# Attention with a bilinear gate in one kernel: when split weights count as ready, when score banks count as free, and where the output weights are split

## The chip, the core and the metric

The kernel runs on one core of a Trainium2 chip. TensorE (PE), VectorE (DVE), ScalarE (ACT), GpSimd (POOL) and SyncE (SP, which only issues transfers here) work side by side and wait for one another through semaphores. The metric is the device time of one execution in microseconds; lower is better.

## The reference

The input x has 2048 rows of 576 values in float32. It is normalised row by row; the result xn goes through 32-head attention (head size 18) and through a bilinear unit of width 4608, and both meet in the output:

```python
    xn = _layernorm(x, axis=-1)
    s = _A_ref(xn, A_wqkv, A_wo)
    g = _silu(_B_ref(xn, B_w_gate, B_w_up, B_w_down))
    return x + s * g
# _A_ref: softmax(q k^T * Dh**-0.5) v, heads joined, @ wo
# _B_ref: h = (x @ w_gate) * (x @ w_up); h @ w_down
```

## The kernel before

**Splitting.** PE multiplies a rounded form of float32 (`fp32r`). To keep accuracy, each operand is split into a high part, which is a rounded copy made by ACT, and a low part, which is the difference, made by POOL or DVE. A product is then the sum of three of the four products of parts. Weights are split on the chip once and the split form is stored to DRAM, so that later passes only load it.

**Stages.** First the rows are normalised and transposed, q and k are computed (`qk_block`) and stored split to `sqk`, and v is computed in blocks of 128 rows (`v_block`): 28 matmuls into two PSUM banks, two ACT copies (L391) into a tile `vo`, and a store of it to `sv` (L393). There are three `vo` tiles, taken in turn. Four v blocks come early, eight later, then six q/k blocks of which the x columns are already on their way to the tile `xc` (L417), and then the last four v blocks.

The main stage runs four passes, one for each 512 rows. A pass has 18 units of 256 columns of the bilinear unit. A unit has two gate/up blocks of 27 matmuls (L618), which multiply x columns with the tile `wgu`, and then eight down blocks (L664), which multiply `hs` with the tile `wd` and add up into `acc`. Up uses one half of the array's rows, gate the other. Between them stand the scores: `a_item` (L530) computes scores of which DVE takes the row maximum (L532), `b_item` (L569) computes them again, transposed, and ACT takes the exponential (L571), and `pv_group` (L580) multiplies with v. Each kind of score has two PSUM banks; the other products share four.

Finally the attention's rows are transposed and multiplied with the output weights (L1187), scaled by the gate and added to x.

**What sets the order.** Everything is ordered by hand while the program is built. A planner keeps two clocks `clk`, one for each half of the array, a time `free` for DVE, ACT and POOL, and for each PSUM bank a time when it comes free. `pick` takes the next gate/up or down matmul that `can_go`, and scores are placed when their goal has come or nothing else can go. A score's bank is counted free 0.06 us after its reader's planned end.

**Small work.** The pieces of weight splitting stand in the list `chores`, other small work (the silu of finished rows) in `later`. At each step `small` may place one of them: for a piece on ACT, only if the planner thinks ACT free within 0.1 us.

```python
                if eng == "POOL" or free[eng] <= now + 0.1 + (0.15 * (now - quiet[0]) if q is later else 0.0):
```

When a block of products is placed whose weights have not been split yet, `gu_start` or `down_start` calls `ready`, which places all pieces ahead of it at once:

```python
    def ready(done, key):
        while key not in done:
            assert chores or later
            chore()
```

In pass 1, `g_get` makes the pieces of a gate/up block (three ACT copies L205, three POOL subtracts L206) and `d_get` those of a unit's down weights (two of each, L236 and L237). Their last entry, `end`, issues the store of the split weights and the load of the next raw ones on SP.

**Output weights.** `wo_prepare` is called with the last gate product. It loads them (L763, L765), and five ACT copies (L771) and five DVE subtracts (L772) split them.

Of the kernel before, what the change touches and what calls it, by code (L numbers as in the profile page):

```python
# [20 lines left out]
FT = mybir.dt.float32  # L21
FR = mybir.dt.float32r
# [18 lines left out]
def kernel(  # L41
# [10 lines left out]
    nc = tc.nc  # L52
# [23 lines left out]
    sv = dram.tile([S, H, DH + 1], FT, name="sv")  # L76
    so = dram.tile([S, D], FT, name="so")
    sg = dram.tile([S, D], FT, name="sg")

    turns = [0]  # L80

# [63 lines left out]


    chores, later = [], []

    def chore(all=True):
        q = (all and chores) or later  # L150
# [30 lines left out]
    def g_get(n):  # L181

        if n == 2 * len(units):
            u = n // 2 - 1
            dw[u] = wpool.tile([128, 2, 2, D], FR, name="wdl", tag="wgu", bufs=2)
            nc.sync.dma_start(dw[u].bitcast(FT), swd[columns_of(u)])
            ddone.add(u)
        if n >= 2 * len(units):
            return
        f = 2 * columns_of(n // 2) + n % 2  # L190
        if n > 1 and n // 2 % NF2 == 0:
            gw[n] = gw[n - 2]
            gdone.add(n)
            return
        w = gw[n] = g_tile()
        if n >= 2 * NF2:
            nc.sync.dma_start(w.bitcast(FT), swg[f])
            gdone.add(n)
            return
        if n not in graw:  # L200
            ready(gdone, n - 2)
        raw = graw.pop(n)

        def piece(b):
            nc.scalar.activation(w[:, b:b + 3, :], raw[:, b:b + 3, :], AF.Copy)  # L205
            nc.gpsimd.tensor_tensor(w[:, 9 + b:12 + b, :], raw[:, b:b + 3, :], w[:, b:b + 3, :].bitcast(FT),  # L206
                                    op=OP.subtract)

        def end():
            gdone.add(n)  # L210
            nc.sync.dma_start(swg[f], w.bitcast(FT))
            g_load(n + 2)

        chores.extend([(piece, (b,)) for b in (0, 3, 6)] + [(end, ())])
# [5 lines left out]
    def d_get(n):  # L220
        if n >= len(units) - 1:
            return
        p = columns_of(n)
        if n and n % NF2 == 0:
            dw[n] = dw[n - 1]
            ddone.add(n)
            return
        w = dw[n] = d_tile()
        if n >= NF2:
            nc.sync.dma_start(w.bitcast(FT), swd[p])  # L230
            ddone.add(n)
            return
        raw = draw.pop(n)

        def piece(k):
            nc.scalar.activation(w[:, k, 0, :], raw[:, k], AF.Copy)  # L236
            nc.gpsimd.tensor_tensor(w[:, k, 1, :], raw[:, k], w[:, k, 0, :].bitcast(FT), op=OP.subtract)  # L237

        def end():
            ddone.add(n)  # L240
            nc.sync.dma_start(swd[p], w.bitcast(FT))
            d_load(n + 1)

        chores.extend([(piece, (k,)) for k in range(2)] + [(end, ())])

    R = 3 * DH
    PT = 13
# [106 lines left out]
                i, k = x_part(b, 0)  # L354
                nc.sync.dma_start(xg[i][r:r + 64, k:k + 2, :].bitcast(FT), sx[c, b])

    vbox = {}

    def v_fetch(h):
        raw = vp.tile([128, 5, HALF], FT, name="wvraw", bufs=1)  # L360
# [7 lines left out]
    def v_split(h):  # L368
        if h == 0:
            vbox["w"] = vp.tile([128, 10, D], FR, name="wv")  # L370
            for i in range(3):
                vbox[i] = vp.tile([128, H, DH + 1], FT, name=f"vo{i}")
                nc.gpsimd.memset(vbox[i], 1.0)
        raw, wv = vbox["raw"], vbox["w"]
        cs = slice(h * HALF, (h + 1) * HALF)
        for k, d, lo in ((0, 0, 4), (1, 1, 5), (2, 2, 6), (3, 3, 7), (4, 8, 9)):
            nc.scalar.activation(wv[:, d, cs], raw[:, k, :], AF.Copy)
            nc.gpsimd.tensor_tensor(wv[:, lo, cs], raw[:, k, :], wv[:, d, cs].bitcast(FT),
                                    op=OP.subtract)

    def v_block(t):
        c, r = divmod(t, 4)
        ps = [bank("g", 3), bank("g", 3)]
        for h in range(2):
            for n, (a, e) in enumerate(PAIRS):
                nc.tensor.matmul(ps[h][:, 0:HALF], xcs[c][:, e, r * 128:(r + 1) * 128],  # L386
                                 vbox["w"][:, a, h * HALF:(h + 1) * HALF], start=n == 0,
                                 stop=n == len(PAIRS) - 1)
        v = vbox[t % 3]
        for h in range(2):  # L390
            nc.scalar.activation(v[:, 16 * h:16 * h + 16, 0:DH],  # L391
                                 ps[h][:, 0:HALF].rearrange("p (a b) -> p a b", b=DH), AF.Copy)
        nc.sync.dma_start(sv[t * 128:(t + 1) * 128], v)  # L393
# [68 lines left out]
    for i in range(2):  # L462
        qs.append(stk.tile([128, S], FR, name=f"qs{i}"))
        ks.append(stk.tile([128, S], FR, name=f"ks{i}"))
        nc.gpsimd.memset(ks[i].bitcast(FT), 1.0)
    g_load(0)
    g_load(1)
    d_load(0)
# [29 lines left out]
    for t in range(4, 8):  # L498
        v_block(t)
        chore()  # L500
    assert n == 18
    pro.close()
    vstack.close()

# [7 lines left out]
    with ExitStack() as mid:  # L512
# [106 lines left out]
                             stop=k == len(TERMS) - 1)  # L619

        def up_end(n, ps):
            us[n] = mp.tile([128, 512], FT, name="us", bufs=1)
            nc.scalar.activation(us[n], ps, AF.Copy)  # L623

# [99 lines left out]
        def down_summed(u, s):  # L724
            c, q = units[u]
            if q == NF2 - 1 and c < NCH - 1:
                seen[c, s] = seen.get((c, s), 0) + 1
                if seen[c, s] == 2:
                    silu_store(4 * c + s)

        def silu(t, new, end):

# [25 lines left out]

        wos = {}

        def wo_prepare():
            raw = xcp.tile([128, 8, D], FT, name="wor", tag="xc")
            nc.sync.dma_start(raw[:, 0:4, :], wo[0:512, :].rearrange("(k p) c -> p k c", p=128))  # L763
            for b in (0, 64):
                nc.sync.dma_start(raw[b:b + 64, 4, :], wo[512:576, :])  # L765
            wos[0] = xcp.tile([128, 8, D], FR, name="wos", tag="xc")
            wos[1] = wpool.tile([128, 2, D], FR, name="wos2", tag="wgu", bufs=2)

            def piece(k):
                hi, lo = (wos[0][:, k, :], wos[0][:, 4 + k, :]) if k < 4 else (wos[1][:, 0, :], wos[1][:, 1, :])  # L770
                nc.scalar.activation(hi, raw[:, k, :], AF.Copy)  # L771
                nc.vector.tensor_tensor(lo, raw[:, k, :], hi.bitcast(FT), op=OP.subtract)  # L772

            chores.extend([(piece, (k,)) for k in range(5)])

        passed = {}

        def stream(r, kind):

            def glu(n):  # L780
                c, q = units[n // 2]
                box = []
                for k in range(len(TERMS)):
                    def work(k=k):
# [6 lines left out]
                        if k == len(TERMS) - 1:  # L791
                            (gate_end if r else up_end)(n, box[0])
                            if r and n == 2 * len(units) - 1:
                                wo_prepare()
                    end = (("DVE", 0.70) if r else ("ACT", 0.60)) if k == len(TERMS) - 1 else None
                    yield 0.229, k == 0, work, end, ("g", n, k), len(TERMS)

# [33 lines left out]
        clk, free = [0.0, 0.0], {"DVE": 0.0, "ACT": 0.0, "POOL": 0.0}  # L831
        banks = {"a": [0.0] * 2, "b": [0.0] * 2, "g": [0.0] * 4}
        turn = {"a": 0, "b": 0}

# [30 lines left out]
        def a_next(r=0):  # L865
# [7 lines left out]
            a_item(h, i, r)  # L873
            slot = turn["a"] % 2
            turn["a"] += 1
            banks["a"][slot] = engine("DVE", clk[r] + 0.45, 0.70) + 0.06
            clk[r] += 0.229
            na += 1
            if i == N - 1:
# [8 lines left out]
        def b_next(r=1):  # L888
# [10 lines left out]
            slot = turn["b"] % 2  # L899
            turn["b"] += 1  # L900
            end = engine("ACT", clk[r] + 0.45, 0.60)
            banks["b"][slot] = end + 0.06
            clk[r] += 0.229
            nb += 1
            if i % 4 == 3:
                due.append((h, i // 4, end + 0.1))

        KINDS = {"piece": ("ACT", 0.55), "first": ("ACT", 0.70), "second": ("DVE", 0.45), "inverse": ("DVE", 1.06)}

        quiet = [0.0]  # L910

        def small(now):

            q = chores or later
            if q is later and now < quiet[0]:
                return
            if q:
                eng, length = KINDS.get(q[0][0].__name__, ("POOL", 0.0))
                if eng == "POOL" or free[eng] <= now + 0.1 + (0.15 * (now - quiet[0]) if q is later else 0.0):
                    if eng != "POOL":  # L920
                        done = engine(eng, now, length)
                        if q[0][0].__name__ == "piece":
                            engine("POOL", done + 0.1, 1.05)
                    elif q[0][0].__name__ == "last":
                        engine("POOL", now, 1.5)
                    if not chores:
                        quiet[0] = now + (16.0 if q[0][0].__name__ == "last" else 6.0)
                    chore()

        def rows(job):  # L930
# [51 lines left out]
        def can_go(r, first, ev):  # L982
# [3 lines left out]
            if kind == "d":  # L986
                if r and not alone(n, k // 6):
                    return k % 6 or handed.get((n, k // 6), 1e9) <= now
                if first and (sum(t >= 1e9 for t in banks["g"]) >= 3 or len(handed) > WAITING):
                    return False  # L990
                return k or (there.get(("h", n), 1e9) <= now and (n < 1 or downed.get(n - 1, 1e9) <= now))
            u = n // 2
            c, q = units[u]
            if k == 0:
                if n > 1 and loaded.get(n - 2, 1e9) > now:
                    return False
                if r and ahead[0] - ahead[1] < FIRST and heads[0]["g"] is not None:
                    return False
# [231 lines left out]
```

## Time and profile before

| | |
|---|---|
| time, median of 3 runs | 2736.94 us (2736.72 to 2739.9) |
| the profiled execution | 2743.11 us, of which the span of its records is 2741.1 us |
| PE busy | 2666.4 us (97%) |
| DVE busy | 1825.9 us (67%) |
| ACT busy | 1571.0 us (57%) |
| POOL busy | 651.9 us (24%) |
| DMA | 428.40 MB, 156 GB/s on the mean |
| mean granted clock of TensorE | 0.986 |

The main stage begins at 216.9 us of the span; its first pass ends near 817 us. In a view by stretches a row has the length of the stretch, then for each engine its busy time and the number of its instructions, then the granted clock of TensorE as a share of full speed, the busy share of the DMA engines and the rate. In a list of waits a row has who waited, for whom, and total, count and longest in microseconds. In a timeline a row has start, length, engine, line and operation, and in brackets the idle time before it and what ended it.

### The profile page before, as it was taken

Reading aid. Unit: us, or ns where it says so; the run is one execution under the profiler, and the core shown is the slowest. Engines: PE = TensorE matmul, PEld = TensorE weight load, DVE = VectorE, ACT = ScalarE, POOL = GpSimd, SP = SyncE. Lnnn points to the kernel's source line nnn. Section 1 sums busy time; section 2 is a strip of 40 time slices with the busy share of each in tenths; the row PEclk is TensorE's granted clock in tenths of the full one; section 3 lists DMA queues with packets and bytes.
Section 4 is the critical chain, followed back from the end, with each engine's and each line's share of the span. In section 5 each row is a group of like instructions: output and inputs, shape, how many; then the busy total and the mean of one; then the engine's idle time right before and its main releaser. Section 6 shows DMA issues by size and latency. Waiting matters only on the chain.

```text
span 2741.1 us, 59194 instructions
## 1 busy us (share of the span) xinstructions
PE 2666.4 (97%) x24504; PEld 2181.3 (80%) x24504; DVE 1825.9 (67%) x3012; ACT 1571.0 (57%) x3096; POOL 651.9 (24%) x671
## 2 busy tenths in 40 slices
PE   7998999989899999999999999999999999999999
PEld 6897887767677887788778778888887888887779
DVE  7207776656566777776677777777777777777336
ACT  4222666656565666566655666666666666666652
POOL 3113534433331111111111112111111122211115
PEclk9999999989899999999999999999999999999999
DMA  7797757756565453544454445444456444443346
GB/s 218 228 288 213 209 152 198 191 147 147 163 155 152 133 149 124 144 131 124 146 137 133 124 151 147 140 140 137 146 138 151 138 144 136 144 144 108 122 141 215
DMA packets 199805, 428.40 MB, mean 156 GB/s; under 512 B 80976, under 2 KB 130544, under 8 KB 166128
## 3 DMA queue, kind: packets, MB, share of 16 engines
q1 hardware_dynamic: 197296, 416.36, 51.4%
q0 software_dynamic: 2240, 8.26, 0.8%
q8 instruction: 192, 3.15, 0.5%
q14 instruction: 77, 0.63, 0.1%
HBM read 311.69 MB, written 107.61 MB: 153 GB/s over the span
## 4 chain that ended last, share of the span: by engine, by line
PE 92%; DMA 3%; DVE 2%; SPq 1%; ACT 1%; POOL 1%; issue 1%; POOLq 0%; ACTq 0%; DVEq 0%
PE pg L618 33%; PE pg L580 17%; PE pg L664 15%; PE pa L530 11%; PE pb L569 9%; PE pg L1187 2%; PE pg L386 2%; PE pa L332 1%; PE pb L332 1%; SPq L417 1%; DMA wgu<-swg 1%; POOL wd L237 1%; DMA ks<-sqk 1%; ACT pt L571 0%; DVE xn L294 0%
## 5 line engine op out<-in xcount | busy, mean ns | idle before, releaser
L532 DVE TENSOR_REDUCE mx<-pa 128x1 f32<-128x512 f32 x2048 | 1374.9, 687 | 350.9 <-PE pa L530 199.9
L618 PE MATMUL pg<-xc,wgu 64*128 64x512 f32 x7776 | 1478.3, 396 | 24.7 <-ACT vo L391 12.3
L571 ACT ACTIVATE pt<-pb 128x512 f32<-128x512 f32 x2048 | 1168.0, 597 | 560.3 <-PE pb L569 399.9
L618 PEld LDWEIGHTS pg<-xc,wgu 64*128 64x128 f32 x7776 | 1093.9, 188 | 70.5 <-ACT vo L391 12.6
L664 PE MATMUL pg<-wd,hs 64*128 64x288 f32 x6816 | 886.5, 297 | 19.9 <-ACT wd L236 10.1
L664 PEld LDWEIGHTS pg<-wd,hs 64*128 64x128 f32 x6816 | 814.9, 188 | 42.5 <-POOL wd L237 14.3
L569 PE MATMUL pb<-qs,ks 56*128 56x512 f32 x2048 | 814.5, 407 | 0.3 <-ACT pt L571 0.2
L530 PE MATMUL pa<-ks,qs 54*128 54x512 f32 x2048 | 809.4, 403 | 0.0
L580 PE MATMUL pg<-pt,vt 128*32 128x512 f32 x4096 | 463.9, 599 | 6.0 <-DVE us L630 2.7
L530 PEld LDWEIGHTS pa<-ks,qs 54*128 54x128 f32 x2048 | 374.8, 186 | 77.7 <-issue 66.2
L640 POOL TENSOR_TENSOR hs<-us,hs 128x512 fp32r<-128x512 f32 x144 | 185.8, 1290 | 991.2 <-ACT hs L633 806.7
L569 PEld LDWEIGHTS pb<-qs,ks 56*128 56x128 f32 x2048 | 372.5, 185 | 25.9 <-ACT pt L571 10.8
L684 POOL TENSOR_TENSOR acc<-acc,st 128x288 f32<-128x288 f32 x268 | 216.2, 808 | 617.2 <-ACT st L715 324.5
L580 PEld LDWEIGHTS pg<-pt,vt 128*32 128x32 f32 x4096 | 123.9, 110 | 288.7 <-issue 272.9
L586 DVE TENSOR_TENSOR oc<-oc,pg 128x512 f32<-128x512 f32 x64 | 44.0, 687 | 306.7 <-PE pg L580 306.7
L633 ACT ACTIVATE hs<-us 128x512 fp32r<-128x512 f32 x144 | 91.0, 632 | 118.9 <-DVE us L630 118.7
L721 DVE TENSOR_TENSOR acc<-acc,pg 128x288 f32<-128x288 f32 x277 | 123.5, 447 | 48.1 <-PE pg L664 43.9
L206 POOL TENSOR_TENSOR wgu<-wraw,wgu 128x384 fp32r<-128x384 f32 x108 | 107.5, 1012 | 195.0 <-ACT wgu L205 145.2
L630 DVE TENSOR_TENSOR us<-pg,us 128x512 f32<-128x512 f32 x144 | 98.7, 685 | 50.0 <-PE pg L618 40.4
L715 ACT ACTIVATE st<-pg 128x288 f32<-128x288 f32 x268 | 109.9, 410 | 37.3 <-PE pg L664 22.8
L623 ACT ACTIVATE us<-pg 128x512 f32<-128x512 f32 x144 | 85.8, 595 | 39.5 <-PE pg L618 34.0
L584 ACT ACTIVATE oc<-pg 128x512 f32<-128x512 f32 x32 | 19.1, 598 | 132.8 <-PE pg L580 132.8
(105 smaller groups left out, 1148.9 us busy)
## 6 DMA issues: line engine op xcount, KB each, us to landing
wgu<-swg SPq DMA_DIRECT2D x102, 1152.0 KB
wd<-swd SPq DMA_DIRECT2D x50, 1152.0 KB
swg<-wgu SPq DMA_DIRECT2D x36, 1152.0 KB
qs<-sqk SPq DMA_DIRECT2D x192, 144.0 KB
ks<-sqk SPq DMA_DIRECT2D x192, 144.0 KB
swd<-wd SPq DMA_DIRECT2D x18, 1152.0 KB
sqk<-hl SPq DMA_DIRECT2D x32, 512.0 KB
xc<-sx SPq DMA_DIRECT2D x48, 256.0 KB
```

What stands on the lines that cost most here:

```text
L206: nc.gpsimd.tensor_tensor(w[:, 9 + b:12 + b, :], raw[:, b:b + 3, :], w[:, b:b + 3, :].bitcast(FT), op=OP.subtract)
L530: nc.tensor.matmul(p, q[rows, t * 128:(t + 1) * 128], k[rows, c * 512:(c + 1) * 512], start=True, stop=True)
L532: nc.vector.tensor_reduce(mx[h][:, t, c:c + 1], p, axis=AX.X, op=OP.max)
L569: nc.tensor.matmul(p, k[rows, t * 128:(t + 1) * 128], q[rows, c * 512:(c + 1) * 512], start=True, stop=True)
L571: nc.scalar.activation(pt[t, c // 2][:, c % 2, :], p, AF.Exp, scale=scale)
L580: nc.tensor.matmul(p[32 * c:32 * c + 32, :], vt[h // 2][:, t, 6 * (h % 2):6 * (h % 2) + 32], pt[t, c // 2][:, c % 2, :], start=t == ts[0], ...
L618: nc.tensor.matmul(ps, gw[n][half[r], a, :], xg[i][half[r], e, :], start=k == 0, stop=k == len(TERMS) - 1)
L640: nc.gpsimd.tensor_tensor(hj[:, 1, :], h32, hj[:, 0, :].bitcast(FT), op=OP.subtract)
L664: op = nc.tensor.matmul(ps[:, 0:HALF], hs[u][half[r], j, a, s * 128:(s + 1) * 128], dw[u][half[r], j, e, i * HALF:(i + 1) * HALF], start=( ...
L684: nc.gpsimd.tensor_tensor(a, a, st, op=OP.add)
L715: nc.scalar.activation(st, ps[:, 0:HALF], AF.Copy)
L721: nc.vector.tensor_tensor(a, a, ps[:, 0:HALF], op=OP.add)
```

## The change

Five things are changed.

- Splitting notes in `split_at` when POOL should be done with a block's low parts. `can_go` does not let the first matmul of a gate/up or down block go before its weights' `end` was placed and that time has come. In `small`, what ACT may still have ahead of it grows by 0.15 us for each us since the last piece was placed, for pieces too. The pieces of down weights get lengths of their own in the planner (`big_piece`).
- A score bank counts as free 0.18 us, not 0.06 us, after its reader's planned end.
- Two more `vo` tiles are made after the first four v blocks, so that later v blocks take five in turn.
- The output weights are split in pass 2, in five steps behind the silu of tile 3: a load into the tile of the down weights' raw form (`draw`, free by then), an ACT copy, two POOL subtracts and two stores to `swo`. With the last gate product the split form is fetched from there.
- `up_end` places the low parts of `hs` that are still pending before it takes the tile `us` anew.

```diff
+    swo = dram.tile([128, 10, D], FT, name="swo")
...
+    clk, free, split_at = [0.0, 0.0], {"DVE": 0.0, "ACT": 0.0, "POOL": 0.0}, {}
...
         def end():
             gdone.add(n)
+            split_at["g", n] = free["POOL"] + 0.2
             nc.sync.dma_start(swg[f], w.bitcast(FT))
             g_load(n + 2)
...
-        def piece(k):
+        def big_piece(k):
...
         def end():
             ddone.add(n)
+            split_at["d", n] = free["POOL"] + 0.2
...
+    def more_rows(pool, n):
+        for _ in range(n):
+            vrows.append(pool.tile([128, H, DH + 1], FT, name=f"vo{len(vrows)}"))
+            nc.gpsimd.memset(vrows[-1], 1.0)
...
-        v = vbox[t % 3]
+        v = vrows[vturn[0] % len(vrows)]
+        vturn[0] += 1
...
+    vmore = ExitStack()
+    more_rows(vmore.enter_context(tc.tile_pool(name="vmore", bufs=1, side="right")), 2)
     g_load(0)
...
         def up_end(n, ps):
+            while lows:
+                pool_now()
...
                 if seen[c, s] == 2:
                     silu_store(4 * c + s)
+                    if 4 * c + s == 3:
+                        for k in range(5):
+                            wo_split(k)
...
-        def wo_prepare():
...
-            def piece(k):
-                hi, lo = (wos[0][:, k, :], wos[0][:, 4 + k, :]) if k < 4 else (wos[1][:, 0, :], wos[1][:, 1, :])
-                nc.scalar.activation(hi, raw[:, k, :], AF.Copy)
-                nc.vector.tensor_tensor(lo, raw[:, k, :], hi.bitcast(FT), op=OP.subtract)
+        def wo_split(k):
+            box = []
+            def fetch():
+                w = wpool.tile([128, 2, D], FR, name="wor", tag="draw", bufs=1)
+                box.append(w)
+                if k < 4:
+                    nc.sync.dma_start(w[:, 0, :].bitcast(FT), wo[128 * k:128 * k + 128, :])
...
+            def whole():
+                nc.scalar.activation(box[0][:, 1, :], box[0][:, 0, :].bitcast(FT), AF.Copy)
+            def rest(i):
+                w = box[0][:, :, i * HALF:(i + 1) * HALF]
+                nc.gpsimd.tensor_tensor(w[:, 0, :], w[:, 0, :].bitcast(FT), w[:, 1, :].bitcast(FT), op=OP.subtract)
+            def keep():
+                for i, j in ((1, k if k < 4 else 8), (0, 4 + k if k < 4 else 9)):
+                    nc.sync.dma_start(swo[:, j, :], box[0][:, i, :].bitcast(FT))
+            later.extend([(fetch, ()), (whole, ()), (rest, (0,)), (rest, (1,)), (keep, ())])
+
+        def wo_fetch():
             wos[0] = xcp.tile([128, 8, D], FR, name="wos", tag="xc")
+            nc.sync.dma_start(wos[0].bitcast(FT), swo[:, 0:8, :])
             wos[1] = wpool.tile([128, 2, D], FR, name="wos2", tag="wgu", bufs=2)
+            nc.sync.dma_start(wos[1].bitcast(FT), swo[:, 8:10, :])
...
-            banks["a"][slot] = engine("DVE", clk[r] + 0.45, 0.70) + 0.06
+            banks["a"][slot] = engine("DVE", clk[r] + 0.45, 0.70) + 0.18
...
-            banks["b"][slot] = end + 0.06
+            banks["b"][slot] = end + 0.18
...
-                if eng == "POOL" or free[eng] <= now + 0.1 + (0.15 * (now - quiet[0]) if q is later else 0.0):
+                if eng == "POOL" or free[eng] <= now + 0.1 + 0.15 * (now - quiet[0] if q is later else now - quiet[1]):
...
+                if k == 0 and (n not in ddone or split_at.get(("d", n), 0.0) > now):
+                    return False
...
-                if n > 1 and loaded.get(n - 2, 1e9) > now:
+                if n not in gdone or split_at.get(("g", n), 0.0) > now or n > 1 and loaded.get(n - 2, 1e9) > now:
                     return False
```

More of the change, by code (lines that the diff above doesn't have):

```diff
@@ L240, in end @@
             ddone.add(n)
+            split_at["d", n] = free["POOL"] + 0.2
             nc.sync.dma_start(swd[p], w.bitcast(FT))
             d_load(n + 1)
-        chores.extend([(piece, (k,)) for k in range(2)] + [(end, ())])
+        chores.extend([(big_piece, (k,)) for k in range(2)] + [(end, ())])
     R = 3 * DH
@@ L355, in x_block @@
                 nc.sync.dma_start(xg[i][r:r + 64, k:k + 2, :].bitcast(FT), sx[c, b])
-    vbox = {}
+    vbox, vrows, vturn = {}, [], [0]
+    def more_rows(pool, n):
+        for _ in range(n):
+            vrows.append(pool.tile([128, H, DH + 1], FT, name=f"vo{len(vrows)}"))
+            nc.gpsimd.memset(vrows[-1], 1.0)
     def v_fetch(h):
@@ L370, in v_split @@
             vbox["w"] = vp.tile([128, 10, D], FR, name="wv")
-            for i in range(3):
-                vbox[i] = vp.tile([128, H, DH + 1], FT, name=f"vo{i}")
-                nc.gpsimd.memset(vbox[i], 1.0)
+            more_rows(vp, 3)
         raw, wv = vbox["raw"], vbox["w"]
@@ L501 @@
     assert n == 18
+    vmore.close()
     pro.close()
@@ L759 @@
         wos = {}
-        def wo_prepare():
[L762 to L765, printed above, removed]
+        def wo_split(k):
[5 more added lines that the diff above has]
+                    nc.sync.dma_start(w[:, 0, :].bitcast(FT), wo[128 * k:128 * k + 128, :])
+                else:
+                    for b in (0, 64):
+                        nc.sync.dma_start(w[b:b + 64, 0, :].bitcast(FT), wo[512:576, :])
+            def whole():
[8 more added lines that the diff above has]
+        def wo_fetch():
             wos[0] = xcp.tile([128, 8, D], FR, name="wos", tag="xc")
+            nc.sync.dma_start(wos[0].bitcast(FT), swo[:, 0:8, :])
             wos[1] = wpool.tile([128, 2, D], FR, name="wos2", tag="wgu", bufs=2)
-            def piece(k):
-                hi, lo = (wos[0][:, k, :], wos[0][:, 4 + k, :]) if k < 4 else (wos[1][:, 0, :], wos[1][:, 1, :])
-                nc.scalar.activation(hi, raw[:, k, :], AF.Copy)
-                nc.vector.tensor_tensor(lo, raw[:, k, :], hi.bitcast(FT), op=OP.subtract)
-            chores.extend([(piece, (k,)) for k in range(5)])
+            nc.sync.dma_start(wos[1].bitcast(FT), swo[:, 8:10, :])
         passed = {}
@@ L793, in work @@
                             if r and n == 2 * len(units) - 1:
-                                wo_prepare()
+                                wo_fetch()
                     end = (("DVE", 0.70) if r else ("ACT", 0.60)) if k == len(TERMS) - 1 else None
@@ L830 @@
         slots, gone = {}, [0.0, 0.0]
-        clk, free = [0.0, 0.0], {"DVE": 0.0, "ACT": 0.0, "POOL": 0.0}
         banks = {"a": [0.0] * 2, "b": [0.0] * 2, "g": [0.0] * 4}
@@ L906, in b_next @@
                 due.append((h, i // 4, end + 0.1))
-        KINDS = {"piece": ("ACT", 0.55), "first": ("ACT", 0.70), "second": ("DVE", 0.45), "inverse": ("DVE", 1.06)}
-        quiet = [0.0]
+        KINDS = {"piece": ("ACT", 0.55), "big_piece": ("ACT", 0.71), "first": ("ACT", 0.70), "second": ("DVE", 0.45), "inverse": ("DVE", 1.06), "whole": ("ACT", 0.71)}
+        quiet = [0.0, 0.0]
         def small(now):
+            if not chores:
+                quiet[1] = now
             q = chores or later
@@ L917, in small @@
             if q:
-                eng, length = KINDS.get(q[0][0].__name__, ("POOL", 0.0))
-                if eng == "POOL" or free[eng] <= now + 0.1 + (0.15 * (now - quiet[0]) if q is later else 0.0):
+                name = q[0][0].__name__
+                eng, length = KINDS.get(name, ("POOL", 0.0))
+                if eng == "POOL" or free[eng] <= now + 0.1 + 0.15 * (now - quiet[0] if q is later else now - quiet[1]):
                     if eng != "POOL":
                         done = engine(eng, now, length)
[L922 to L927, printed above, removed]
+                        if name in ("piece", "big_piece"):
+                            engine("POOL", done + 0.1, 1.05 if name == "piece" else 1.47)
+                    elif name in ("last", "rest"):
+                        engine("POOL", now, 1.5 if name == "last" else 0.85)
+                    if chores:
+                        quiet[1] = now
+                    else:
+                        quiet[0] = now + (16.0 if name == "last" else 6.0)
                     chore()
```

## The prediction

> **What bounds the kernel now.** I read the page first, for the engine that leads and when it does not, then a table of stretches, then PE's waits in the bad stretch, then the timeline around single waits.
>
> ```profile
> PE 2666.4 (97%) x24504; PEld 2181.3 (80%) x24504; DVE 1825.9 (67%) x3012; ACT 1571.0 (57%) x3096; POOL 651.9 (24%) x671
> PE   7998999989899999999999999999999999999999
> PEclk9999999989899999999999999999999999999999
> PE 92%; DMA 3%; DVE 2%; SPq 1%; ACT 1%; POOL 1%; issue 1%; POOLq 0%; ACTq 0%; DVEq 0%
> ```
>
> PE holds 92% of the chain, so whatever shortens the run must let PE start earlier, idle less or run at a higher granted clock. DVE and ACT have room on average. The slices below 9 lie in the first third, which is the start and pass 1. Stretches say it in numbers:
>
> ```profile
> core 0: us, PE busy (x) PEld busy (x) DVE busy (x) ACT busy (x) POOL busy (x), PEclk, DMA share, GB/s
> 204.00:217.00 13.00, 0.68 (x6) 0.45 (x4) 0.00 (x0) 0.89 (x3) 0.00 (x0) 0.66 0.68 204
> 217.00:222.00 5.00, 5.00 (x24) 5.00 (x26) 2.15 (x4) 0.01 (x1) 0.00 (x0) 0.52 0.96 289
> 300.00:900.00 600.00, 567.13 (x5185) 449.05 (x5183) 386.28 (x627) 373.57 (x740) 215.06 (x208) 0.95 0.60 164
> 734.00:747.40 13.40, 10.47 (x55) 9.20 (x57) 4.26 (x7) 4.67 (x9) 5.66 (x6) 0.50 0.59 201
> 900.00:1500.00 600.00, 596.48 (x5710) 480.30 (x5708) 439.16 (x717) 364.79 (x706) 106.68 (x110) 1.00 0.45 136
> 1600.00:2200.00 600.00, 599.74 (x5844) 489.36 (x5842) 443.16 (x722) 371.31 (x721) 108.53 (x112) 1.00 0.47 142
> ```
>
> From 300 to 900 us, mostly pass 1, PE finishes 5185 matmuls; later stretches of the same length finish 5710 and 5844 of nearly the same mix. Two losses stand in the row: 32.9 us of idle PE and a mean granted clock of 0.95. Who causes the idle time:
>
> ```profile
> PE pg L664 <- ACT wd L236: 10.1, 8, 2.3
> PE pg L664 <- POOL wd L237: 9.9, 11, 1.1
> PE pg L618 <- ACT wgu L205: 6.7, 5, 2.5
> PE pg L618 <- DMA xc<-sx: 2.2, 2, 1.8
> PE pg L618 <- POOL wgu L206: 2.1, 5, 0.6
> ```
>
> These are PE's waits between 300 and 900 us (total, times, longest). 28.8 us are waits for the pieces in which weights are split, and splitting happens in pass 1 alone. One such wait closely:
>
> ```profile
> 731.89 1.28 ACT L236 ACTIVATE wd<-draw 128x576 fp32r<-128x576 f32 x2
> 732.64 0.39 PE L664 MATMUL pg<-wd,hs 64*128 64x288 f32 x1 [1.53 <-ACT wd L236]
> 732.73 2.77 POOL L237 TENSOR_TENSOR wd<-draw,wd 128x576 fp32r<-128x576 f32 x2 [10.53 <-ACT wd L236]
> 734.19 0.60 PE L664 MATMUL pg<-wd,hs 64*128 64x288 f32 x1 [1.05 <-POOL wd L237]
> 741.14 0.79 PE L618 MATMUL pg<-xc,wgu 64*128 64x512 f32 x1 [2.46 <-ACT wgu L205]
> ```
>
> POOL had idled 10.5 us: nothing was too slow, the two ACT pieces merely stood in ACT's queue just ahead of the down product that needs them. The code says why. `small` lets a piece in only when the planner thinks ACT free within 0.1 us, which a stream of exponentials seldom allows; when the down product is placed, `ready` empties the list, pieces and matmul go out together, and PE waits behind its own order.
>
> **The change, part by part.**
>
> *Weights counted as ready.* `can_go` now holds back the first matmul of a gate/up or down block until its `end` has been placed and POOL's planned time has passed; the planner puts scores there instead. With it `small` lets an overdue piece in after ever more ACT backlog (0.15 us per us waited). No instruction is added; ACT's and POOL's pieces only move forward in their queues. Behind a moved pair of `wd` pieces wait exponentials, for 1.28 us (row 731.89), on an engine busy 374 of 600 us; POOL is busy 215 of 600. The stores and raw loads that `end` issues on SP's queue move forward with the pieces, where pass 1 has no weight loads of the other kind to pass. The price of the old way has two bounds by matmul counts: 5185 matmuls at the rate of 900–1500 us take 5185/5710 x 600 = 544.8 us, a loss of 55.2; at the rate of 1600–2200 us 532.3, a loss of 67.7. The two losses of the row, 32.9 idle and 0.05 x 600 = 30 of clock, make 62.9 and agree. I take 58, nearer to the pass next door, and 40 to 68 as bounds, since some waits (the x columns, 2.2 us) stay. What is late next: if scores run out, banks; at the pass boundaries the new program has placed 5223, 11118 and 16993 matmuls, the old one 5221, 11045 and 17005, so nothing is pushed into later passes.
>
> The clock is half of this sum, so it needs its own reasoning. The row 734–747.4 shows a granted clock of 0.50 for 13.4 us, after gaps of 1.53 and 1.05 us and with one of 2.46 us inside. So here a group of short gaps costs more in clock than in idle time. The Trainium skill, "TensorE: Matmul & The Clock Gate", section "What's actually happening", has the array fall to half clock after at least one idle window of about 3.4 us. By that rule none of the gaps of pass 1, at most 2.46 us, would cost clock, and the gain would be their idle time alone. This trace disagrees: no wait in the list above is longer than 2.5 us, and the stretch runs at 0.95. The measurement decides, and the other reading is a rival below.
>
> *Two more v tiles.*
>
> ```profile
> 201.07 2.84 SPq L417 DMA_DIRECT2D xc<-xcx  x4
> 207.54 9.62 SPq L393 DMA_DIRECT2D sv<-vo  x4
> 216.11 0.71 ACT L391 ACTIVATE vo<-pg 128x288 f32<-128x288 f32 x2 [14.41 <-DMA sv<-vo]
> 216.87 0.79 PE L618 MATMUL pg<-xc,wgu 64*128 64x512 f32 x1 [12.32 <-ACT vo L391]
> L373 POOL MEMSET vo<- 128x608 f32 x3 | 1.7, 595 | 0.0
> ```
>
> The last v block needs the tile of the block three before it, whose store was issued at 207.54 behind loads on SP's queue; ACT's copy waits 14.4 us and holds the PSUM banks that the first gate product needs. With five tiles, it needs the tile of the block five before it, which belongs to the earlier run of v blocks, ahead of six q/k blocks, and is long stored. PE can then go on about 1 us after its v block, so 12.3 − 1 = 11.3 us go. What could be late next are the last x columns, whose fetch SP issued until 203.9; the v store of 207.54 took 8.6 us to land, so at worst they land near 212.5, and the last terms of the first product, some 60 matmuls at 600/5844 = 0.10 us after a start at 205.6, want them at 212. Bounds 8 to 12.3. The half clock after the gap (217–222: 0.52) goes as well: 5 x 0.48 = 2.4, bounds 0 to 2.4. Two more memsets are 1.2 us of POOL, and lie where POOL waits for ACT; nothing.
>
> *Score banks free 0.12 us later in the plan.* This only moves scores.
>
> ```profile
> PEld pb L569 <- ACT pt L571: 7.2, 40, 0.2
> ```
>
> Between 900 and 2650 us PE waited 7.2 us for score banks that the plan had counted free too early; that is the most to be gained there. The cost is a score placed later, perhaps with a gap before it; no row shows it. Bounds −7 and +15; I take +3, since the pass counts above hardly move.
>
> *Output weights split in pass 2.*
>
> ```profile
> L236 ACT ACTIVATE wd<-draw 128x576 fp32r<-128x576 f32 x36 | 23.6, 684 | 0.0
> L684 POOL TENSOR_TENSOR acc<-acc,st 128x288 f32<-128x288 f32 x268 | 216.2, 808 | 617.2 <-ACT st L715 324.5
> 2655.95 0.75 DVE wos L772
> 2659.13 1.72 DVE wos L772 x3
> 2667.85 3.97 PE pg L1187 x28
> PE pg L664 <- DVE acc L721: 1.0, 2, 0.8
> 2640.00:2650.00 10.00, 10.00 (x105) 8.93 (x108) 1.63 (x4) 8.91 (x18) 2.09 (x2) 1.00 0.73 275
> ```
>
> Added: 5 ACT copies at 0.68 = 3.4 us, 10 POOL subtracts at 0.81 = 8.1 us, and 4.4 MB of DMA, on engines with that room in pass 2. They stand in `later` behind the silus of tiles 0 to 3, and the next silus come only at the end of pass 2, so nobody waits for them there; but their loads and stores are queued on SP ahead of gate and down loads, so a late POOL subtract could hold one of those: 0 to +3, I take +1. Removed at the end: five ACT and five DVE pieces, of which the chain of waits holds 0.75 + 1.72 = 2.5 us between the last down products; PE's own waits for DVE at that place are 1.0 us. I take −1.7, bounds 0 and −2.5. In their place the split weights, 2.95 MB, are fetched at about 2645; at the 275 GB/s of the last row that is 10.7 us, done near 2658 with the landing, ten before the first output product at 2667.85.
>
> *`up_end` empties `lows` first.* It changes POOL's order by a place; nothing.
>
> **The sum**, against the profiled execution's 2743.1 us (span 2741.1): −58 − 11.3 − 2.4 + 3 + 1 − 1.7 = −69.4, so 2673.7. The median shown is 2736.9, 6.2 below that execution; the same gain gives **2667.5 us**. With the terms' bounds: 2645 to 2690.
>
> **The rivals.**
>
> *The clock does not come back* (the skill's reading, or other short gaps that keep it low): idle time alone goes, −32.9 − 11.3 + 3 + 1 − 1.7 = −41.9, so 2695. For it: the rows do not separate what each single gap costs in clock. Against: 900–1500 us has 3.5 us of gaps and stands at 1.00. Chance 0.08.
>
> *The v tiles change nothing*, because the x columns or another load hold the first product just as long: −69.4 + 13.7 = −55.7, so 2681. For it: the DMA share is 0.68 and 0.96 around the start. Against: the row names the v copy alone. Chance 0.11.
>
> *The weights stay late*, since pieces still go out last on ACT: only the start and the small terms, −11.3 − 2.4 + 2.3 = −11.4, so 2725.5. Against: the hold in `can_go` makes the order itself wait. Chance 0.07.
>
> *Slower: the loose plan costs more than the waits.* Each of 4096 scores is kept from its bank 0.12 us longer. If nothing else were at hand, that is 491 us of one array half, 246 us of both. It outweighs 72 us of gain from the point where 30% of the scores find nothing else to stand before them; at 40% the time is 2737 + 98 − 72 = 2763. For it: the first matmuls are now also held back, so fewer fillers exist. Against: the score banks made PE wait only 7.2 us in 1750, so they are seldom the limit, and blocks of 27 and 48 products are long fillers. Chance 0.06.
>
> **How the numbers follow.** The forecast has 0.68. The range 2645 to 2700 holds nearly all of it and the first two rivals, about 0.85. This kernel's time can be told from no change from about 0.2%, 5.5 us, on. The forecast and the first two rivals are faster by more (0.87), and nearly all of the third (0.05 of its 0.07); its rest is within 0.2% (0.02); the last is slower (0.06).
>
> **What would show it.** Right: PE's slices at 9 from the sixth on; no wait of PE for `wd` or `wgu` over a few us in total between 290 and 850 us; granted clock 0.99 or more there; some 5700 matmuls in 600 us; the first gate product near 206 us; no `wos` copies at the end, and the first output product not waiting for the fetch. Wrong: waits for weights of 10 us or more in pass 1, a clock of 0.95 without gaps, the first gate product past 214 us, or clearly fewer than 5700 matmuls per 600 us from 900 us on, which would be the last rival.

## The result, and the profile after

| | before | changed |
|---|---|---|
| median | 2738.14 us (2736.72 to 2739.9, 4 runs) | 2663.11 us (2662.34 to 2663.43, 4 runs) |
| ratio, with 95% interval | | 0.9725 (0.9708 to 0.9742) |
| span of the profiled execution | 2741.1 us | 2661.7 us |
| mean granted clock | 0.986 | 0.999 |

The change is 75 us faster; 2667.5 was predicted. The page after, engines and slices, and by engine the chain that ended last:

```profile
PE 2634.4 (99%) x24504; PEld 2148.6 (81%) x24504; DVE 1820.2 (68%) x3007; ACT 1568.5 (59%) x3096; POOL 663.9 (25%) x683
PE   7999999999999999999999999999999999999999
PEclk9999999999999999999999999999999999999999
PE 97%; DVE 2%; DMA 1%; ACT 0%; POOL 0%; issue 0%; SPq 0%; POOLq 0%; ACTq 0%; DVEq 0%
```

Only the first slice is below 9 now. The stretches of the prediction, taken at the same times:

```profile
core 0: us, PE busy (x) PEld busy (x) DVE busy (x) ACT busy (x) POOL busy (x), PEclk, DMA share, GB/s
204.00:217.00 13.00, 12.93 (x110) 11.02 (x110) 9.78 (x15) 3.08 (x7) 1.86 (x2) 1.00 0.92 290
300.00:900.00 600.00, 598.52 (x5783) 476.78 (x5783) 428.43 (x700) 403.70 (x800) 224.21 (x216) 1.00 0.64 178
900.00:1500.00 600.00, 598.14 (x5731) 476.94 (x5725) 447.29 (x729) 381.31 (x736) 110.49 (x115) 1.00 0.47 143
1600.00:2200.00 600.00, 599.78 (x5834) 484.15 (x5832) 446.57 (x725) 369.10 (x717) 107.65 (x111) 1.00 0.47 139
2562.00:2572.00 10.00, 10.00 (x86) 6.07 (x86) 0.69 (x1) 5.62 (x10) 1.66 (x2) 1.00 0.92 358
```

From 300 to 900 us PE finishes 5783 matmuls where it finished 5185; idle time fell from 32.9 to 1.5 us, and the clock rose from 0.95 to 1.00. The last row is the fetch of the split output weights, at 358 GB/s. All of PE's waits from 204 to 892 us (who, for whom, total, count, longest):

```profile
PE pg L591 <- DVE acc L734: 1.0, 2, 0.6
PE pg L677 <- ACT st L728: 0.7, 1, 0.7
PE pg L591 <- DVE us L643: 0.3, 1, 0.3
PE pb L580 <- DMA qs<-mr: 0.3, 1, 0.3
```

Not one is for a weight. POOL's group of down pieces between 290 and 860 us, first before, then after, tells where they went: POOL's idle time ahead of them that an ACT piece ended fell from 51.7 to 26.3 us, so they are spread out rather than placed late.

```profile
L237 POOL TENSOR_TENSOR wd<-draw,wd 128x576 fp32r<-128x576 f32 x30 | 42.1, 1419 | 66.4 <-ACT wd L236 51.7 <-issue 10.1 <-DMA swg<-wgu 4.5
```

```profile
L240 POOL TENSOR_TENSOR wd<-draw,wd 128x576 fp32r<-128x576 f32 x30 | 42.7, 1428 | 26.8 <-ACT wd L239 26.3 <-ACT mr L565 0.2
```

The start, in the timeline after (a score stands first now, then the first gate product):

```profile
204.72 0.50 PE L541 MATMUL pa<-ks,qs 54*128 54x512 f32 x2
204.83 0.41 ACT L399 ACTIVATE vo<-pg 128x288 f32<-128x288 f32 x1 [1.43 <-PE pg L393]
205.29 1.41 PE L629 MATMUL pg<-xc,wgu 64*128 64x512 f32 x9
```

Where the 79.4 us between the two spans came from, by the first gate product of each pass in the two traces:

| stage | before | changed | difference |
|---|---|---|---|
| up to the first gate product | 216.9 | 205.3 | −11.6 |
| pass 1 | 599.8 | 543.4 | −56.4 |
| pass 2 | 625.7 | 622.4 | −3.3 |
| pass 3 | 615.2 | 607.0 | −8.2 |
| pass 4, to the last down product | 609.0 | 609.0 | 0 |
| output | 74.6 | 74.6 | 0 |

### The profile page after: what moved, and what is told of

The parts are those of the page before. It is cut to its first block, busy times and chain, and to the rows that moved or that the text cites. A ratio compares the mean times of both kernels' runs of the same rounds, so it can differ in the third digit from the quotient of the medians.

```text
span 2661.7 us, 59233 instructions
## 1 busy us (share of the span) xinstructions
PE 2634.4 (99%) x24504; PEld 2148.6 (81%) x24504; DVE 1820.2 (68%) x3007; ACT 1568.5 (59%) x3096; POOL 663.9 (25%) x683
## 4 chain that ended last, share of the span: by engine, by line
PE 97%; DVE 2%; DMA 1%; ACT 0%; POOL 0%; issue 0%; SPq 0%; POOLq 0%; ACTq 0%; DVEq 0%
PE pg L629 35%; PE pg L591 17%; PE pg L677 16%; PE pa L541 11%; PE pb L580 9%; PE pg L1226 2%; PE pg L393 2%; PE pa L336 2%; PE pb L336 2%; DVE xn L298 0%; DVE mx L543 0%; DVE st L287 0%; PE pb L1203 0%; DMA sqk<-hl 0%; PE pg L319 0%; DMA qs<-mr 0%
## 5 line engine op out<-in xcount | busy, mean ns | idle before, releaser
L629 PE MATMUL pg<-xc,wgu 64*128 64x512 f32 x7776 | 1444.1, 392 | 0.1
L629 PEld LDWEIGHTS pg<-xc,wgu 64*128 64x128 f32 x7776 | 1075.2, 186 | 68.0 <-issue 6.7
L677 PE MATMUL pg<-wd,hs 64*128 64x288 f32 x6816 | 854.9, 294 | 0.7 <-ACT st L728 0.7
L580 PE MATMUL pb<-qs,ks 56*128 56x512 f32 x2048 | 805.2, 401 | 0.4 <-DMA qs<-mr 0.3
L677 PEld LDWEIGHTS pg<-wd,hs 64*128 64x128 f32 x6816 | 790.6, 185 | 17.2 <-issue 2.5
L580 PEld LDWEIGHTS pb<-qs,ks 56*128 56x128 f32 x2048 | 370.8, 184 | 13.2 <-issue 2.9
```

What stands on the lines that cost most here:

```text
L580: nc.tensor.matmul(p, k[rows, t * 128:(t + 1) * 128], q[rows, c * 512:(c + 1) * 512], start=True, stop=True)
L629: nc.tensor.matmul(ps, gw[n][half[r], a, :], xg[i][half[r], e, :], start=k == 0, stop=k == len(TERMS) - 1)
L677: op = nc.tensor.matmul(ps[:, 0:HALF], hs[u][half[r], j, a, s * 128:(s + 1) * 128], dw[u][half[r], j, e, i * HALF:(i + 1) * HALF], start=( ...
```

## The experiments

Differences to the changed kernel are between medians. Its own runs lie within 1.1 us, and the intervals reach some 4 us to either side, so less than about 5 us is not told apart. The kernel before, run again beside each group of experiments, had medians of 2734.9 to 2739.4 us; a difference between runs of different groups is less sure by as much.

**What ends the stalls: the hold or the allowance?** First the hold taken out of `can_go`, then instead the larger allowance of `small`:

```diff
-                if k == 0 and (n not in ddone or split_at.get(("d", n), 0.0) > now):
-                    return False
...
-                if n not in gdone or split_at.get(("g", n), 0.0) > now or n > 1 and loaded.get(n - 2, 1e9) > now:
+                if n > 1 and loaded.get(n - 2, 1e9) > now:
```

> The changed kernel without the hold: a gate/up or down block may be placed before its weights' pieces, as before; the larger ACT allowance for overdue pieces stays. Theory A (the hold is what ends the stalls): pieces are forced out together with the products that need them again, PE waits for wd and wgu 20 us or more in pass 1 with clock lost beside it, and the time returns by 40 to 58 us to about 2703 to 2721. Theory B (the allowance alone places pieces in time, the hold seldom acts): within 8 us of 2663, and under 5 us of PE waits for weights.

Measured: 2666.06 us, 3 slower, ratio to before 0.9733 (0.9718 to 0.9747). PE's waits for weights over the whole main stage:

```profile
PE pg L677 <- POOL wd L240: 2.0, 2, 1.0
PE pg L677 <- ACT wd L239: 1.3, 2, 0.8
```

3.3 us, not 20 or more. Theory A is refuted, theory B holds: with the allowance the pieces go out in time nearly always, and without the hold PE still meets a late one only four times.

```diff
-                if eng == "POOL" or free[eng] <= now + 0.1 + 0.15 * (now - quiet[0] if q is later else now - quiet[1]):
+                if eng == "POOL" or free[eng] <= now + 0.1 + (0.15 * (now - quiet[0]) if q is later else 0.0):
```

> The changed kernel with the hold, but a piece is let in only when ACT is planned free within 0.1 us, as before. Theory A: no PE waits for weights, but products are held back while pieces wait for a free ACT, so scores run ahead and PE idles or the later passes get more of the gate work; 5 to 30 us slower than 2663. Theory B (the allowance is the whole gain): 40 us or more slower, about 2710. A third reading, that the hold alone is enough because held products leave room on ACT: within 5 us of 2663.

Measured: 2803.48 us, 140 slower, and slower than before: 1.0235 (1.0218 to 1.0252). That is far beyond every reading on record. Pass 1 takes 773 us, 543 in the changed kernel, and holds 1281 scores instead of 885; passes 2 to 4, which are left with fewer, give 90 us back. Its row, and PE's two largest waits in it:

```profile
300.00:900.00 600.00, 586.00 (x4500) 398.29 (x4500) 399.27 (x642) 381.14 (x735) 168.00 (x162) 0.89 0.47 128
```

```profile
PE pb L580 <- ACT pt L582: 5.6, 17, 0.5
PE pa L541 <- DVE mx L543: 4.5, 12, 0.8
```

No wait is for a weight: the order keeps the products back and puts scores in, and the scores wait for their two banks. PE looks 98% busy and does 4500 matmuls where the changed kernel does 5783, at a clock of 0.89. So the hold without the allowance is worse than the stalls that it avoids. As the code reads, pieces wait until the planner sees ACT free, products wait for pieces, and each transposed score put in their place books ACT again; no run takes this apart further.

**The v tiles.** The two extra tiles are left out (`more_rows` for `vmore`, and its `close`).

> The changed kernel with three v tiles instead of five. If the start was held by the v copy alone, the first product moves from 204.7 back to about 216.9 us and the clock falls to half behind the gap: 12.2 + 2.4 = 14 to 15 us slower, about 2677.5. If something else would have held the start as long, under 4 us slower.

Measured: 2674.93 us, 11.8 slower (13.2 between the profiled spans); 14 to 15 were expected. The first gate product stands at 216.5 us, and the wait is back:

```profile
PE pg L626 <- ACT vo L399: 11.0, 1, 11.0
```

The v copy alone held the start.

**The score banks.** The constant is varied, here back to 0.06:

```diff
-            banks["a"][slot] = engine("DVE", clk[r] + 0.45, 0.70) + 0.18
+            banks["a"][slot] = engine("DVE", clk[r] + 0.45, 0.70) + 0.06
...
-            banks["b"][slot] = end + 0.18
+            banks["b"][slot] = end + 0.06
```

> The changed kernel with score banks counted free 0.06 us after the planned end, as before. Forecast's reading (the number only moves scores, the net is +3 us): 0 to 5 us faster than 2663. Rival reading, from passes 2 and 3 of the changed kernel, which are 11.5 us shorter than before although the forecast gave them +4: the banks count is where they gain, by orders without matmuls that wait behind a full bank; then 8 to 15 us slower, and PE's weight loads wait for exponentials again by 5 us or more in total between passes 2 and 4, where the changed kernel's list has 1.0 us.

> The changed kernel with the banks counted free 0.30 us after the planned end. If each further 0.12 us only moves scores: within 4 us of 2663. If the plan gets loose, as the slower rival had it: 10 us slower or more, with fewer matmuls in 600 us of the later passes (5835 in the changed kernel). If waits behind full banks are still there at 0.18: 3 us faster or more.

> The changed kernel with the banks counted free 0.12 us after the planned end, between 0.06 (2694) and 0.18 (2663). If a full bank that the plan thinks free is a steady cost, the weight loads' waits for exponentials (10.3 us at 0.06, 0.6 at 0.18) lie between, 2 to 7 us, and the time too, 2668 to 2685. If most of the 31 us is an accident of one order (x columns or row maxima that come just too late, each followed by half clock), the time need not lie between; it then follows the sum of such single gaps, and the waits for exponentials still lie between.

> The changed kernel with the banks counted free 0.24 us after the planned end, between 0.18 (2663) and 0.30 (2708). Accident reading: waits for exponentials stay under 5 us, and the time is 2665 plus whatever single gaps of over 1 us the order happens to have (at 0.30 it had gaps of 11.4 and 9.8 us and scores left over for the end); within 15 us of 2663 without such gaps. Steady reading (each 0.12 us loosens the plan): halfway, 2680 to 2690, without large gaps.

| constant | time | PE's weight loads waiting for exponentials, 205 to 2690 us | what else PE waited for, over 2 us at once |
|---|---|---|---|
| 0.06 | 2693.82 us | 10.3 us, 49 times | x columns 2.8, rows of o 2.1 |
| 0.12 | 2658.54 us | 0.2 us | none |
| 0.18 | 2663.11 us | 0.6 us | none |
| 0.24 | 2685.77 us | 0.6 us | x columns 4.1, row maxima 3.4, `hs` 2.2 |
| 0.30 | 2707.65 us | 6.7 us, 17 times | row maxima 11.4, rows of o 9.8 |

The rows behind the two ends of the table, for 0.06 and for 0.30:

```profile
PEld pb L580 <- ACT pt L582: 10.3, 49, 1.0
PE pg L629 <- DMA xc<-sx: 5.0, 3, 2.8
750.00:772.00 22.00, 19.21 (x149) 14.25 (x146) 11.55 (x21) 10.70 (x21) 2.56 (x2) 0.86 0.96 224
```

```profile
PE pb L580 <- DMA qs<-mr: 11.4, 1, 11.4
PE pb L1203 <- DMA oin<-so: 9.8, 1, 9.8
```

The waits behind full banks are gone at 0.12 already, and between 0.06 and 0.12 the time falls by 35 us. Those waits are at most 10 us of it: weight loads overlap with matmuls (busy 81% of that span beside PE's 99%), and PE itself stood still for exponentials only 1.1 us. More comes through the order: at 0.06 the first x columns of pass 2 come 2.8 us late and the clock around that gap falls to 0.86.

At 0.30 the two gaps make 21.2 us, and half clock while PE was busy costs another 11 (half of the time that the records of the granted clock have at half clock with PE busy): about 32 of the 43.6 us between the profiled spans. The stages show where: passes 1 to 3 are 26 us shorter than in the changed kernel, pass 4 is 47 longer and the output 23. The order has put scores off: 1083 of them stand in pass 4 instead of 975, and six between the output's products. So here the loss is largely one of scores left for the end, where little stands beside them. At 0.24, whose four runs lie 12 us apart, the three gaps make 9.7 us and the clock of 0.997 some 5, 15 of 22.7.

The steady reading fits neither 0.12, which is as fast as 0.18, nor 0.24, which has large gaps. The accident reading fits these two: each value makes another order, in which other loads come just too late. For 0.30 it is not shown, since scores put off are what a loose plan does. The rest of the differences was not taken apart.

**The output weights.** `wo_prepare` is put back for `wo_split` and `wo_fetch`.

> The changed kernel with the output weights loaded and split at the end, as before, and nothing of them in pass 2. Forecast's terms: +1 in pass 2 and -1.7 at the end, so 0.7 us slower, about 2664. Rival (the end before was held longer than its waits show, or pass 2 is fuller than thought): more than 4 us off to either side.

Measured: 2656.49 us, 6.6 faster than the changed kernel, 0.9711 (0.9696 to 0.9725) of before; that interval and the one of the changed kernel overlap. Pass 2 takes 622.8 us against 622.4 and the output 74.6 in both, so neither place of the split shows. Passes 3 and 4 are 1.6 and 7.8 us shorter, by another order. At the end, PE's waits between down products are back at their small size:

```profile
PE pg L677 <- DVE acc L734: 1.8, 2, 1.5
```

**Single parts on the kernel before.** The weights part alone, and the banks' 0.18 alone. Both have the fifth change, the low parts of `hs` placed first, which no run tests by itself:

> The kernel before with only the weights part: the hold, the allowance for overdue pieces, the lengths of the down pieces, and the low parts of hs placed ahead of a new us. Forecast: -58 of 2738, about 2680, with the wait of 12 us at the start still there. If the parts need each other (banks and weights): 2695 or more.

> The kernel before with only the score banks counted free 0.18 us after the planned end (the low parts of hs placed ahead of a new us, and pieces of the output weights left over when the order ends placed at once). Forecast: +3, about 2741. If the banks carry a gain of their own in the later passes: 8 to 15 us faster, about 2725; if the loose plan costs: 2745 or more.

Weights alone: 2712.83 us, 22 faster than the 2734.93 of the runs beside it, 0.9906 (0.9888 to 0.9924). No wait for weights is left and pass 1 is 42 us shorter, but the order loses elsewhere, and passes 2 to 4 are 12 us longer:

```profile
PE pg L621 <- ACT vo L394: 12.3, 1, 12.3
PE pg L621 <- DMA xc<-sx: 6.7, 4, 2.4
PE pg L669 <- DVEq L673: 2.7, 1, 2.7
PE pb L572 <- DMA qs<-mr: 2.6, 1, 2.6
```

Banks alone: 2764.43 us, 29.5 slower, 1.0103 (1.0086 to 1.012). Passes 2 to 4 are shorter than before here too (1811.7 us against 1849.9), but pass 1 takes 639 us, because more pieces go out late, and the end waits for the last rows of o:

```profile
PE pg L618 <- ACT wgu L205: 16.2, 12, 2.2
PE pg L666 <- POOL wd L237: 14.6, 17, 1.1
PE pg L666 <- ACT wd L236: 13.6, 11, 2.0
PE pg L618 <- POOL wgu L206: 6.7, 12, 0.6
PE pb L1168 <- DMA oin<-so: 10.5, 1, 10.5
```

51.1 us of waits for weights, where the kernel before had 28.8 between 300 and 900 us. So the parts do not add: −22, +29.5 and some −12 for the v tiles would make −4, and together they make −75. With the pieces on time, the slack at the banks gains; with late pieces it costs. Why more pieces go out late with it is not shown.

**What a short gap costs in clock.** In pass 3 of the changed kernel, PE is made to wait about 2 us once per unit, by ACT copies in place that change no value:

```diff
             ready(ddone, u)
+            if r == 0 and u // NF2 == 2 and u not in stalled:
+                stalled.add(u)
+                for _ in range(2):
+                    nc.scalar.activation(dw[u][:, 0, 0, :], dw[u][:, 0, 0, :].bitcast(FT), AF.Copy)
```

> The changed kernel with two ACT copies in place (0.68 us each, of values that do not change by them) on the down weights just ahead of the first down product of each of the 18 units of pass 3, so that PE waits about 1.5 to 2 us there, 18 times, in a stretch that had full clock. If only idle of 3.4 us or more costs clock: 18 times the gap and nothing else, 27 to 36 us slower, granted clock 1.00 in pass 3. If short gaps cost clock as pass 1 before suggested (30 us of clock beside 33 of idle): 45 to 70 us slower, clock 0.95 to 0.98 in pass 3.

Measured: 2722.57 us, 59.5 slower. PE's waits and the row of pass 3 (the 18th gap, 2.0 us, lies just behind this stretch), then pass 3 of the changed kernel:

```profile
PE pg L683 <- ACT wd L677: 35.1, 17, 2.3
1371.00:2040.00 669.00, 633.83 (x5961) 507.12 (x5959) 454.14 (x739) 403.05 (x773) 112.19 (x115) 0.97 0.44 131
```

```profile
1371.00:1978.00 607.00, 606.78 (x5889) 487.67 (x5887) 447.12 (x729) 373.76 (x728) 110.80 (x113) 1.00 0.47 141
```

The gaps make 35.1 + 2.0 = 37.1 us. The clock of 0.97 over 669 us makes 20 more, and the sum of 57 comes near the 59.5. The loss of clock is not spread evenly: the records of the granted clock have 3.41 us at half clock behind 11 of the 18 gaps, 1.7 us lost each time and 18.8 in all, and none behind the other seven. A stretch behind the first gap, then one behind the second:

```profile
1438.00:1441.50 3.50, 3.50 (x42) 3.47 (x40) 2.17 (x4) 2.44 (x5) 0.04 (x1) 1.00 0.23 36
1470.40:1473.70 3.30, 3.30 (x22) 3.23 (x22) 2.08 (x3) 1.27 (x3) 0.00 (x0) 0.50 0.00 0
```

No gap was longer than 2.3 us. The first reading (27 to 36 us at full clock) is refuted.

**The two faster versions in one.** 0.12 with the output weights split at the end:

> Both versions that came out below the changed kernel's 2663 in one: banks counted free 0.12 us after the planned end (2658.5 alone) and the output weights split at the end (2656.5 alone). If the two gains are of a steady kind they add up: about 2652. If each of them is the luck of its own order of instructions, the sum says nothing, and the time lies anywhere within some 10 us of 2660; single gaps of over 1 us in PE then tell which.

Measured: 2673.82 us, 15 and 17 slower than the two. One large gap in PE stands out, near the end of the down products, where a hand-over between the array's halves was put behind work on DVE:

```profile
PE pg L677 <- DVEq L681: 8.4, 1, 8.4
```

The chain of work that ended last names that work. It is the splitting of the output weights, which waits for their load:

```profile
2573.78 7.97 DMA wor<-in_A_wo_dram
2581.78 0.69 ACT wos L784
2582.49 0.04 DVE wos L785
```

With the half clock behind it (2.3 us) the gap makes 10.7 of the 15 us to the 0.12 version; the rest was not taken apart. So the two gains do not add and belong to their orders, and splitting at the end can cost 8 us where the order is unlucky. The early split has no such hold, since it leaves no splitting on DVE at the end. No version is shown to beat the changed kernel by more than the intervals allow.

## Why the prediction was right, and where it was not

*The time.* 2667.5 predicted, 2663.1 measured; −69.4 against −75.0. That the sum came so near is in part luck. It adds up terms that do not add: the weights part, −58 in the sum, brings −22 alone, and the banks, +3 in the sum, bring −31 beside the other parts. The two errors nearly cancel.

*The clock is half of the sum in pass 1.* Right, and shown by the gaps put into pass 3: they cost more than half their length again. In pass 1 of the kernel before, the trace has 22.1 us of loss by half clock while PE was busy, beside 28.0 us of idle time; 0 and 2.5 are left in the changed kernel. That is 47.6 of the 56.4 us; the rest was not taken apart, but the mix of work differs too: pass 1 now holds 37 fewer scores and 75 more down matmuls. The sentence of the Trainium skill that was weighed there ("TensorE: Matmul & The Clock Gate", "What's actually happening": half clock after at least one idle window of about 3.4 us) would have had the 37.1 us cost 37.1; they cost 59.5. The rival that hung on it falls.

*Weights counted as ready, −58.* Right in size only in company: pass 1 became 56.4 us shorter, which includes the 2.4 us of clock after the start, listed apart; alone, the part made pass 1 42 us shorter and the kernel 22. The mechanism had the wrong agent. The prediction had the hold in `can_go` make the order wait and named it against the rival of late weights. Without the hold 3 us come back, which is not told apart from nothing; without the allowance the time is 140 us longer. The allowance is the step; the hold is useful at most in a few places, and only beside it.

*The v tiles, −11.3 and −2.4.* Right: the start moved by 11.6 us and its clock is full; undone, 11.8. The x columns did not hold the first product, so that rival falls.

*Score banks, +3 with bounds −7 and +15.* Here the step failed, the one on what the constant does. The bound was read from a wait of 7.2 us in the old order, but the constant changes the whole order. In this kernel 0.06 instead of 0.18 costs 31 us, on the kernel before 0.18 costs 29.5. The stages show it too: passes 2 and 3 lost 11.5 us where the forecast had +4 for all of it. The slower rival was a real danger: at 0.30 in place of 0.18 the time is 44.5 us longer, though by scores put off to the end, with gaps and half clock there, not by a loss on each score.

*Output weights, +1 and −1.7.* Not told apart from nothing. Pass 2 does not show them, the output stage is 74.6 us in both, and the fetch, at 358 GB/s, came in time. What the old way can cost shows in the run with both faster versions, where the split at the end held PE for 8.4 us.

## What to carry to other kernels

When PE waits for small preparing work, look at when that work was let into its engine's queue before making anything faster or holding anything back: POOL had been idle for 10 us ahead of the piece that it was late with. A wait in an ordered program bounds what its removal gains only if the order stays; a constant in a planner changes the order everywhere, so its price is taken by running several values, and a gain of a few us from one value is not a property of it. Where the clock follows activity as here, count gaps of 2 us as some 3 on the mean. When several parts of a change are priced apart, try one or two alone before trusting the sum.

## What the runs showed of the hardware that was not expected

Gaps of 1.8 to 2.3 us, one each 30 to 40 us, lower the granted clock of TensorE to 0.97 on the mean. In the run with the stalls the half-clock stretches begin at whole multiples of 3.41 us from one another. Laid on that raster, each of the 11 gaps with half clock behind it has 1.83 us or more within one step, and none of the other seven more than 1.79. So there it was not the length of a gap that decided, but how it fell on the raster. The bound is that of this one dense stretch. In pass 1 of the kernel before, 1.4 us of idle time in one step was enough (near 359 us), and the waits there often come in pairs: gaps of 1.05 and 0.98 us at 812.1 and 813.7 us, then half clock from 815.7 to 819.1.

The clock also falls with hardly any gaps. With the hold and no allowance, PE was idle 14 us between 300 and 900 us, 1.1 us at most at a time, and the granted clock was 0.89, in a stretch that did 4500 matmuls instead of 5783. One piece of it, in which nearly all matmuls are scores that take turns with their banks:

```profile
335.00:348.60 13.60, 13.60 (x43) 7.06 (x45) 10.62 (x16) 10.15 (x18) 1.00 (x1) 0.50 0.16 37
```

PE is busy throughout by the profile, and the clock is at half. No run separates what the sparse work does from what the short gaps just ahead of it do.
